# Gated attention and squared-ReLU MLP on one core: the exponent's shift from the first 512 keys, and the front part's steps in another order

## The chip, the cores and the metric

The kernel runs on 1 core of one Trainium2 chip. The metric is the device time of one execution in microseconds (us), as the median of several runs.

## The reference, cut to what matters

```python
x = A_x                                             # 1 x 2048 x 512
g = sigmoid((x * gate_w).sum(-1, keepdims=True))
q = (x @ wq) as 32 heads of 16;  k = x @ wk;  v = x @ wv      # one k and v for all heads
scores = einsum("bhqd,bkd->bhqk", q, k) * 16 ** -0.5
a = einsum("bhqk,bkd->bhqd", softmax(scores), v) @ wo
b = relu(x @ w1 + b1) ** 2 @ w2 + b2
out = g * a + (1 - g) * b
```

All of it is float32. wq and wk are drawn some 36 times larger than the other weights, so the scores spread widely.

## The kernel before, in words

The softmax does not look for the largest score of each row. It subtracts a bound, |q| times the greatest key norm, inside the score product itself: the key tile `k_aug` has, beside 3 x 16 rows of the key, a row RS = 32 that holds minus that norm (`km`), and the query tile `qa` has |q| in the same row. Both come twice, in partitions 0 to 48 and 64 to 112, for two heads side by side. A root is a guess from the exponent's bits (`k_max`, `root`). At the end the kernel tests whether every row's sum lay between `L_MIN` and `L_MAX` (2^-80 and 2^64); if one did not, `exact_shift` computes the attention anew.

The long middle part is an order of TensorE's work written by hand and by a planner. A *span* (`Span`, `fetch`) is one unit of products (a tile of queries, a hidden tile of the MLP, a sum): 12 or 15 matmuls in two halves of 64 rows. The second half of a unit runs beside the first half of the next, and each span starts a new PSUM bank `mm` (two of them). A *phase* places a few scores among the products by a text from `PLANS` (M a product, S0 a score block, 02 and 12 the two halves of a score block that goes through the PSUM bank `x` and is copied by VectorE). After each phase `context` multiplies finished exponentials with the values (`v_ext`, line 963). ScalarE turns scores into exponentials (line 943); VectorE copies, splits numbers into two float32r parts and takes units out of PSUM. `soon` lists VectorE's steps that are due early; `spend` lets them out when the planner's clock says that they fit.

The change is in the front part, lines 592 to 651, and in the first phase (`FIRST_PHASE`, line 62, and `last_rows`, line 653). For each chunk c of 512 keys:

- `kv_sums(c)`: x times wk and wv (four matmuls beside each other), then `kv_copy(c)` to SBUF on ScalarE.
- `k_rows(c)`: a matmul that spreads the keys into the rows of `k_aug`; `k_round(c)` rounds them (`kb`), `k_parts(c)` writes `k_aug` on VectorE; `k_shift(c)` then writes -km into row RS of both halves.
- `kv_gather(c)`, `kv_keep(c)`, `kv_turn(c)`: four small matmuls, a copy to SBUF and a transpose that put keys and values with one key a partition, in the PSUM bank `acc`. From there `k_squares` and `k_max` take the greatest norm, and `v_rows` writes `v_ext`.

The first query unit is made early (`q_early`); its rows go to `qa[0]` by small DMAs (`q_direct`) from the SP and POOL queues, and its norms (`qnorm`) as the last of them. `wq_load(2, 2)` loads the last two of the four tiles of wq, which `wq_round` and `wq_rest` split.

Two waits matter later. Each score block holds one of two PSUM buffers `s` until its exponential is done. And after the first phase a one-column copy on VectorE, `peek` (line 1394), reads the bank of the first span; TensorE's next products into that bank come behind it:

```python
        phase(span.slots, AHEAD + 2, 0)
        nc.vector.tensor_copy(at.tile([128, 1], F32, name="peek"), span.bank[:, :1])
        evicted = True
```

Of the kernel before, what the change touches and what calls it, by code (L numbers as in the profile page):

```python
# [10 lines left out]
F32 = mybir.dt.float32  # L11
# [11 lines left out]
NC, CH = 4, 512  # L23
# [37 lines left out]
}  # L61
FIRST_PHASE = "S0 M K M S1 M M M 02 M S3 M M M S4 M 12 M M S5", (0, 1, 3, 4, 5, 2)
HC = CH // 2

Q_ROWS = (0, 0, DH), (DH, 0, DH), (RS + 1, 1, DH), (RS, 2, 1)
FRONT_A, FRONT_V = 8, 22
LAST_OK = NC * KT - 1
# [105 lines left out]
def mix_kernel(ctx: ExitStack, tc: tile.TileContext, xT, xs, gw, wkv, wq, wo, w12, b1, b2, cst, out):  # L173
# [67 lines left out]
    with fast, tc.tile_pool(name="at", bufs=1) as at, \  # L241
# [43 lines left out]
        ones = at.tile([96, 128], BF, name="ones")  # L285
        kmx = at.tile([128, NK], F32, name="kmx")
        kmt = at.tile([128, 1], F32, name="kmt")
# [7 lines left out]
        for i in range(FRONT_V):  # L295
# [3 lines left out]
        ks = {}  # L299
        rows_of = {0: lambda: two[:, 0], 1: lambda: late_kv[:, 1], 2: aside,  # L300
                   3: lambda: mp.tile([128, CH], F32, name="mm")}
        kvt = [at.tile([128, 2, CH], F32, name="kvc", tag="e", bufs=10) for _ in range(2)]
# [3 lines left out]
        def kv_sums(c, parts=range(KT)):  # L306

            if parts[0] == 0:
                kvq[c] = late_kv[:, 0] if c == 3 else aside() if c == 1 else mp.tile([128, CH], F32, name="mm")
            for k in parts:  # L310
                nc.tensor.matmul(kvq[c][32 * k:32 * k + 32], wkvf[:, k], xf[c, k], start=True, stop=True,
                                 skip_group_check=True, tile_position=(0, 32 * k))
# [24 lines left out]

        ks2 = []
        kvg, gathered = [], {}

        def kv_gather(c):

            gathered[c] = mp.tile([128, CH], F32, name="mm") if c % 2 else aside()
            for j in range(4):
                nc.tensor.matmul(gathered[c][32 * j:32 * j + 32, :128], cs[:, C_SEL:C_SEL + 2 * DH],
                                 kvc[c][:, j * 128:(j + 1) * 128], start=True, stop=True,
                                 skip_group_check=True, tile_position=(0, 32 * j))

        def kv_keep(c):
            if not kvg:  # L350
                kvg.append(of_tile("kvg", F32))
            nc.scalar.activation(kvg[0][:, c * 128:(c + 1) * 128], gathered[c][:, :128], AF.Copy)

        def kv_turn(c):
            nc.tensor.transpose(acc[:, c * 128:(c + 1) * 128], kvg[0][:, c * 128:(c + 1) * 128], ident)

        def k_squares(i, n):
            if not ks2:
                ks2.append(of_tile("ksq", F32)[:, :NK * DH].rearrange("p (i d) -> p i d", i=NK))
            ksq = ks2[0]  # L360
            k = kvp[:, i:i + n, :DH]
            nc.scalar.activation(ksq[:, i:i + n], k, AF.Square)
            nc.vector.tensor_reduce(kmx[:, i:i + n], ksq[:, i:i + n], AX.X, OP.add)

        def k_max():
            nc.vector.tensor_reduce(kmt, kmx, AX.X, OP.max)
            pn = mp.tile([128, CH], F32, name="mm")
            nc.tensor.matmul(pn[:, :128], kmt.to_broadcast([128, 128]), ident, start=True, stop=True)

            def rest():  # L370
                nc.vector.tensor_reduce(km, pn[:, :128], AX.X, OP.max)
                nc.vector.tensor_scalar(km.bitcast(I32), km.bitcast(I32), 0.5, ROOT, op0=OP.mult, op1=OP.add)

            return rest

# [23 lines left out]
        def q_early():  # L399
            q = mp.tile([128, CH], F32, name="mm")  # L400
            mm(q, q_terms(0, 0))
            qr, ql = of_tile("qr"), of_tile("ql")

            def rest():
                nc.vector.tensor_tensor(ql, q, qr.bitcast(F32), OP.subtract)
                nc.vector.tensor_tensor(sq8[:, 0], qr.bitcast(F32), qr.bitcast(F32), OP.mult)

            return qr, ql, (lambda: nc.scalar.activation(qr, q, AF.Copy)), rest
# [26 lines left out]
        def qnorm(tiles, p8=None):  # L435
# [4 lines left out]
            for i, (it, sq) in enumerate(tiles):  # L440
                nc.tensor.matmul(p8[32 * i:32 * i + 32], blk, sq, start=True, stop=True, tile_position=(0, 32 * i))  # L441
            nrm, tmp = of_tile("nrm"), of_tile("tmp", F32)
            root(nrm[:n], p8[:n], tmp[:n])
            if tiles[0][0] == 0:
                q_direct(RS, nrm, 1, (nc.sync, nc.gpsimd))
            for i, (it, sq) in enumerate(tiles):
                nc.sync.dma_start(qs[2][it:it + 2].rearrange("u r d a n -> (u r d a) n"),
                                  nrm[32 * i:32 * i + 8].bitcast(F32))
                done.update((it, it + 1))
# [152 lines left out]
        x_pair(1, 0)  # L602
        kv_sums(1)
        two = sp.tile([128, 2, CH], F32, name="s")
        k_rows(0)
        nc.scalar.activation(xr[1][:, 2:], xw[1, 1], AF.Copy)  # L606
        q_round()
# [3 lines left out]
        q_direct(RS + 1, ql, DH, (nc.sync, nc.gpsimd))  # L611
        wq_load(2, 2)
        kv_copy(1)
        kv_gather(0)
        k_round(0)
        kv_keep(0)
        k_parts(0)
        kv_sums(2)
        qnorm([(0, sq8[:, 0])], mp.tile([128, CH], F32, name="mm"))
        kv_copy(2)  # L620
        acc = ap.tile([128, CH], F32, name="acc")
        kvp = acc.rearrange("p (i d) -> p i d", i=NK)
        kv_turn(0)
        kv_gather(1)
        kv_keep(1)
        kv_gather(2)
        kv_keep(2)
        nc.vector.tensor_tensor(xl[1][:, 2:], xw[1, 1], xr[1][:, 2:].bitcast(F32), OP.subtract)
        late_kv = sp.tile([128, 2, CH], F32, name="s")
        kv_sums(3)  # L630
        kv_copy(3)
        kv_turn(1)
        kv_turn(2)
        k_squares(0, 12)
        kv_gather(3)
        kv_keep(3)
        kv_turn(3)
        k_squares(12, 4)
        wq_round(1)
        k_rows(1)  # L640
        norm = k_max()
        nc.vector.tensor_copy(wqr[:, 2], wqf[2])
        k_rows(2)
        k_round(1)
        norm()
        k_shift(0, True)
        k_parts(1)
        k_round(2)
        k_parts(2)
        wq_rest(1)  # L650
        q_write(0, 0, qr, ql, nc.sync)

        def last_rows():

            nonlocal at_pe
            k_rows(3)
            k_round(3)
            k_parts(3)
            at_pe += 0.8
            act(0.6)  # L660
            dve(0.75)

        held, begun = 0.0, [0]
        chores, divisions = [], []
        soon = [(1, 0.7, lambda: wq_rest(2)), (1, 0.9, lambda: k_shift(1)), (1, 0.4, v_rows),
                (1, 0.7, lambda: (act(0.64), wq_round(3), wq_rest(3))), (2, 0.9, lambda: k_shift(2)), (3, 0.9, lambda: k_shift(3)),
# [630 lines left out]
        def phase(slots, n, m):  # L1297
# [23 lines left out]
            for i in range(len(rows[0])):  # L1321
                for r in range(2):
# [3 lines left out]
                    elif item == "K":  # L1326
                        if r == 0:
                            last_rows()
                    elif item[0] == "S":
# [157 lines left out]
```

## Time and profile before

| | |
|---|---|
| median of 3 runs | 1173.27 us (1173.03 to 1173.36) |
| the profiled execution | 1173.4 us, span 1171.8 us |
| TensorE (PE) busy | 1163.3 us, 99% |
| ScalarE (ACT) busy | 1022.9 us, 87% |
| VectorE (DVE) busy | 687.1 us, 59% |
| GpSimd (POOL) busy | 67.7 us, 6% |
| granted TensorE clock, mean | 0.999 |

The profile is of one execution. A timeline row gives the start and the length of one or several like instructions, and in square brackets how long the engine stood idle before and what ended that. Lines such as L906 are lines of the kernel. "PEld" are the weight loads of TensorE. A row with "POOLq" or "SPq" is a transfer issued from that queue; a row of the DMA view ends with the time from issue to landing, where the trace has it.

### The profile page before, as it was taken

How to read it: one execution, taken by the hardware profiler on the slowest of the kernel's cores; microseconds unless marked ns; L12 is line 12 of the kernel's file. 1: busy time of each engine (PE TensorE's matmuls, PEld its weight loads, DVE VectorE, ACT ScalarE, POOL GpSimd, SP SyncE). 2: the span in 40 equal slices, each digit the busy share in tenths (PEclk: the TensorE clock that was granted, in tenths of full speed). 3: DMA queues.
4: the chain of work that ended last, by engine and by line, in shares of the span. 5: the costliest groups of instructions: out<-in, count | busy, mean ns of one | idle time of the engine just before them, and what ended most of it. 6: DMA issues, size and time to landing. Idle time of an engine off the chain costs nothing.

```text
span 1171.8 us, 31969 instructions
## 1 busy us (share of the span) xinstructions
PE 1163.3 (99%) x13791; PEld 778.7 (66%) x13791; DVE 687.1 (59%) x1175; ACT 1022.9 (87%) x1142; POOL 67.7 (6%) x125
## 2 busy tenths in 40 slices
PE   8999999999999999999999999999999999999998
PEld 4666666676666666666666666666666666666665
DVE  6877886764754745553666636535556537544554
ACT  7789999999988888888888888989888889888885
POOL 1000111010100000100000000001000000001000
PEclk9999999999999999999999999999999999999999
DMA  7245535251533513320433305224115224222101
GB/s 265 98 156 175 183 114 195 92 197 45 176 119 121 180 39 121 110 81 20 151 104 143 95 22 180 92 66 157 62 47 168 79 66 136 92 75 92 56 38 39
DMA packets 49290, 130.26 MB, mean 111 GB/s; under 512 B 11350, under 2 KB 11846, under 8 KB 48632
## 3 DMA queue, kind: packets, MB, share of 16 engines
q1 hardware_dynamic: 37272, 90.68, 23.8%
q0 software_dynamic: 11728, 37.43, 8.8%
q8 instruction: 109, 1.79, 0.6%
q14 instruction: 37, 0.30, 0.1%
q10 hardware_dynamic: 144, 0.07, 0.0%
HBM read 87.92 MB, written 35.64 MB: 105 GB/s over the span
## 4 chain that ended last, share of the span: by engine, by line
PE 97%; DMA 1%; ACT 1%; SPq 0%; DVE 0%; issue 0%
PE acc L963 39%; PE mm L1270 34%; PE s L906 19%; PE x L906 5%; DMA xf<-in_xT 1%; DMA wqf<-in_wq 0%; ACT e L943 0%; DVE ot L1230 0%; SPq L413 0%; PE s L212 0%; SPq L268 0%; ACT xr L606 0%; PE mm L320 0%; PE x L1052 0%; PE x L441 0%
## 5 line engine op out<-in xcount | busy, mean ns | idle before, releaser
L943 ACT ACTIVATE e<-s 128x1024 f32<-128x1024 f32 x765 | 747.8, 1023 | 102.5 <-PE s L906 99.4
L927 DVE COPY e<-x 128x512 f32<-128x512 f32 x518 | 358.3, 692 | 445.0 <-PE x L906 275.9
L963 PE MATMUL acc<-e,v_ext 128*32 128x256 f32 x8192 | 470.2, 381 | 0.0
L906 PE MATMUL s<-qa,k_aug 49*128 49x512 f32 x1530 | 407.3, 410 | 0.5 <-DVE k_aug L336 0.3
L963 PEld LDWEIGHTS acc<-e,v_ext 128*32 128x32 f32 x8192 | 252.3, 110 | 193.1 <-issue 40.6
L943 ACT ACTIVATE e<-e 128x1024 f32<-128x1024 f32 x259 | 272.7, 1055 | 0.2 <-ACT e L943 0.2
L906 PEld LDWEIGHTS s<-qa,k_aug 49*128 49x128 f32 x1530 | 214.3, 184 | 85.1 <-ACT e L943 38.8
L1270 PE MATMUL mm<-w2p,hr 64*128 64x512 f32 x1128 | 242.1, 392 | 0.0
L906 PE MATMUL x<-qa,k_aug 49*128 49x512 f32 x518 | 213.5, 412 | 0.0
L1270 PEld LDWEIGHTS mm<-w2p,hr 64*128 64x128 f32 x1128 | 160.4, 186 | 18.5
L1270 PE MATMUL mm<-xragain,w1p 64*128 64x512 f32 x448 | 119.7, 392 | 0.0
L906 PEld LDWEIGHTS x<-qa,k_aug 49*128 49x128 f32 x518 | 95.2, 184 | 35.8 <-DVE e L927 19.8
L1270 PE MATMUL mm<-xr,w1p 64*128 64x512 f32 x448 | 114.8, 392 | 0.0
L1270 PEld LDWEIGHTS mm<-xragain,w1p 64*128 64x128 f32 x448 | 70.2, 186 | 6.7
L1270 PEld LDWEIGHTS mm<-xr,w1p 64*128 64x128 f32 x448 | 68.5, 186 | 6.9
L1270 PE MATMUL mm<-xlagain,w1p 64*128 64x512 f32 x224 | 69.6, 396 | 0.0
L1270 PE MATMUL mm<-xl,w1p 64*128 64x512 f32 x224 | 66.4, 393 | 0.0
L1270 PE MATMUL mm<-more 64*128 64x512 f32 x216 | 60.4, 394 | 0.0
L1017 ACT ACTIVATE accs<-acc 128x256 f32<-128x256 f32 x60 | 23.1, 384 | 28.8 <-PE acc L963 27.1
L789 DVE TENSOR_SCALAR big<-mm,b1t 128x512 f32<-128x512 f32 x56 | 41.6, 742 | 0.0
L790 DVE TENSOR_TENSOR big<-big 128x512 f32<-128x512 f32 x56 | 38.8, 692 | 1.9
L1270 PEld LDWEIGHTS mm<-xlagain,w1p 64*128 64x128 f32 x224 | 35.8, 186 | 4.0
(195 smaller groups left out, 804.0 us busy)
## 6 DMA issues: line engine op xcount, KB each, us to landing
w1p<-w1kept SPq DMA_DIRECT2D x42, 512.0 KB
w2p<-w2kept SPq DMA_DIRECT2D x35, 512.0 KB
qa<-qs SPq DMA_DIRECT2D x186, 64.0 KB
w1kept<-w1p POOLq DMA_DIRECT2D x14, 512.0 KB, 3.7
w2kept<-w2p POOLq DMA_DIRECT2D x12, 512.0 KB, 5.5
qs<-qr SPq DMA_DIRECT2D x16, 256.0 KB
ress<-res POOLq DMA_DIRECT2D x4, 1024.0 KB, 5.5
qs<-ql POOLq DMA_DIRECT2D x15, 256.0 KB, 3.7
```

Of the source, the lines that this page charges most:

```text
L789: nc.vector.tensor_scalar(h[0], p, b1t[:, f:f + 1], 0.0, op0=OP.add, op1=OP.max)
L790: nc.vector.tensor_tensor(h[0], h[0], h[0], OP.mult)
L906: nc.tensor.matmul(dst.rearrange("p (a n) -> p a n", a=2), k_aug[rows, kt * 128:(kt + 1) * 128], qa[it][rows, :, q * HC:q * HC + HC], star ...
L927: nc.vector.tensor_copy(e_half(u)[:, 2 * r:2 * r + 2], x.rearrange("p (a n) -> p a n", a=2))
L943: nc.scalar.activation(e_half(u), src, AF.Exp, scale=SCALE)
L963: nc.tensor.matmul(accs[q][h * 32:(h + 1) * 32], v_ext[:, kt], es[u][:, h % 2 * 2 + h // 2], start=kt == 0 and it > 0, stop=kt == NK - 1, ...
L1017: nc.scalar.activation(a[:, q * HC:q * HC + HC], acc, AF.Copy)
L1270: nc.tensor.matmul((self.before if r else self).bank, a[p], b[p], start=not r and i == 0, stop=r == 1 and i == len(self.terms[1]) - 1, ski ...
```

## The change

The greatest key norm is taken of the first chunk only, so `km` needs chunk 0 alone. In the front part only chunk 0 is gathered, kept and turned; chunks 1 to 3 are gathered, kept and turned inside the first phase, at two new places K of its text. The norms of the first queries come ahead of the root of the key norm. `wq_load(2, 2)` moves behind the norms' DMA on the SP queue. Three steps go from ScalarE to VectorE (the copy of the gathered chunks 1 to 3, the rounding of chunk 3's keys, the rounding of wq's tile 1), and VectorE's split of x's second chunk (`xl[1][:, 2:]`) moves from the front part into `soon`. The short fillers at the start are 5 instead of 8 on ScalarE and 20 instead of 22 on VectorE.

```diff
-FIRST_PHASE = "S0 M K M S1 M M M 02 M S3 M M M S4 M 12 M M S5", (0, 1, 3, 4, 5, 2)
+FIRST_PHASE = "S0 M M K S1 M M M 02 M S3 M K M M S4 M 12 M M K S5", (0, 1, 3, 4, 5, 2)
-FRONT_A, FRONT_V = 8, 22
+FRONT_A, FRONT_V = 5, 20
...
-        def k_squares(i, n):
...
+        def k_squares():
+            ksq = kvg[:, CH - 4 * DH:].rearrange("p (i d) -> p i d", i=4)
+            nc.scalar.activation(ksq, kvp[:, :4, :DH], AF.Square)
+            nc.vector.tensor_reduce(kmx, ksq, AX.X, OP.add)
             nc.vector.tensor_reduce(kmt, kmx, AX.X, OP.max)
...
+        def k_norm():
+            pn = acc[:, CH - 128:]
+            nc.tensor.matmul(pn, kmt.to_broadcast([128, 128]), ident, start=True, stop=True)
+            return pn
+
+        def k_root(pn):
+            nc.vector.tensor_reduce(km, pn, AX.X, OP.max)
+            nc.vector.tensor_scalar(km.bitcast(I32), km.bitcast(I32), 0.5, ROOT, op0=OP.mult, op1=OP.add)
...
+            if tiles[0][0] == 0:
+                k_squares()
             nrm, tmp = of_tile("nrm"), of_tile("tmp", F32)
             root(nrm[:n], p8[:n], tmp[:n])
             if tiles[0][0] == 0:
                 q_direct(RS, nrm, 1, (nc.sync, nc.gpsimd))
+                wq_load(2, 2)
...
         k_rows(0)
+        kv_gather(0)
...
-        wq_load(2, 2)
+        kv_keep(0, 1, scalar_copy)
+        k_round(0)
+        kv_sums(1)
+        kv_turn(0)
+        qnorm([(0, sq8[:, 0])])
         kv_copy(1)
...
+        pn = k_norm()
+        kv_sums(2)
+        kv_copy(2)
+        k_root(pn)
         k_parts(0)
...
+        k_shift(0, True)
         late_kv = sp.tile([128, 2, CH], F32, name="s")
+        k_rows(1)
+        k_round(1)
         kv_sums(3)
         kv_copy(3)
...
+        late_ks = mp.tile([128, CH], F32, name="mm")
+        nc.vector.tensor_copy(wqr[:, 1], wqf[1])
+        wq_rest(1)
         k_rows(2)
...
             k_rows(3)
-            k_round(3)
+            kb[3] = of_tile("kb")
+            nc.vector.tensor_copy(kb[3], ks[3])
             k_parts(3)
...
+        def v_gather():
+
+            for c in range(1, NC):
+                kv_gather(c)
+            kv_keep(1, 3, nc.vector.tensor_copy)
+
+        def v_turn():
+
+            for c in range(1, NC):
+                kv_turn(c)
+            v_rows()
+
+        aside_steps = [last_rows, v_gather, v_turn]
...
-        soon = [(1, 0.7, lambda: wq_rest(2)), (1, 0.9, lambda: k_shift(1)), (1, 0.4, v_rows),
+        soon = [(1, 0.7, lambda: (nc.vector.tensor_copy(wqr[:, 2], wqf[2]), wq_rest(2))),
+                (1, 0.9, lambda: k_shift(1)),
+                (1, 0.4, lambda: nc.vector.tensor_tensor(xl[1][:, 2:], xw[1, 1], xr[1][:, 2:].bitcast(F32), OP.subtract)),
...
-                            last_rows()
+                            aside_steps.pop(0)()
```

How the instructions stand on the engines, first TensorE between the early query unit and the first score block (`s<-qa,k_aug`). `mm<-xk,wkvf` and the like are `kv_sums`, `s<-kvc,cs` is `k_rows`, `32x128 x4` a `kv_gather`, `acc<-cs,kvg` a `kv_turn`, `cs,kmt` the norm. Before, behind `kv_sums(1)`, `k_rows(0)`, `kv_gather(0)`, `kv_sums(2)`, the queries' norms and `kv_turn(0)`:

```order
L345 MATMUL mm<-kvc,cs 32x128 x4
L345 MATMUL x<-kvc,cs 32x128 x4
L311 MATMUL s<-xk,wkvf 32x512 x4
L355 MATMUL acc<-cs,kvg 128x128 x2
L345 MATMUL mm<-kvc,cs 32x128 x4
L355 MATMUL acc<-cs,kvg 128x128
L320 MATMUL s<-kvc,cs 128x512
L368 MATMUL mm<-cs,kmt 128x128
L320 MATMUL x<-kvc,cs 128x512
L906 MATMUL s<-qa,k_aug 128x512 x2
```

And of the change, behind `k_rows(0)`:

```order
L340 MATMUL acc<-kvc,cs 32x128 x4
L310 MATMUL mm<-xf,wkvf 32x512 x4
L348 MATMUL acc<-cs,kvg 128x128
L430 LDWEIGHTS blk
L430 MATMUL x<-sq_172,blk 32x512
L358 MATMUL acc<-cs,kmt 128x128
L310 MATMUL mm<-xk,wkvf 32x512 x4
L319 MATMUL s<-kvc,cs 128x512
L310 MATMUL mm<-xk,wkvf 32x512 x4
L319 MATMUL x<-kvc,cs 128x512
L903 MATMUL s<-qa,k_aug 128x512 x2
```

The norm now stands ahead of the sums of chunks 2 and 3 and ahead of the rows of chunks 1 and 2, and three gathers and three transposes have left this place.

Second, VectorE from the last `k_parts` (`k_aug<-kb,cs,mm`) to `peek`. Before:

```order
L327 SCALAR_TENSOR_TENSOR k_aug<-kb,cs,mm 128x512
L564 TENSOR_TENSOR wql<-wqf,wqr 128x512
L927 COPY e<-x 128x512
L336 TENSOR_SCALAR k_aug<-km 1x512 x2
L927 COPY e<-x 128x512
L1394 COPY peek<-mm 128x1
```

And of the change, from the rounding of chunk 3's keys (`kb<-mm`, on ScalarE before) on:

```order
L638 CAST kb<-mm 128x512
L326 SCALAR_TENSOR_TENSOR k_aug<-kb,cs,mm 128x512
L660 CAST wqr<-wqf 128x512
L556 TENSOR_TENSOR wql<-wqf,wqr 128x512
L924 COPY e<-x 128x512
L345 COPY kvg<-acc 128x384
L335 TENSOR_SCALAR k_aug<-km 1x512 x2
L662 TENSOR_TENSOR xl_91<-xf,xr_87 128x1024
L924 COPY e<-x 128x512
L366 COPY v_ext<-acc 128x256
L1391 COPY peek<-mm 128x1
```

Five instructions that stood elsewhere, or on ScalarE, now stand ahead of `peek`.

Third, VectorE behind `peek`. Before (the copy to `v_ext` ahead of these rows):

```order
L564 TENSOR_TENSOR wql<-wqf,wqr 128x512
L336 TENSOR_SCALAR k_aug<-km 1x512 x4
L204 CAST xr_88<-xk 128x512
L205 TENSOR_TENSOR xl_92<-xk,xr_88 128x512
L422 CAST qr<-mm 128x512
L423 TENSOR_TENSOR ql<-mm,qr 128x512
```

And of the change:

```order
L556 TENSOR_TENSOR wql<-wqf,wqr 128x512
L335 TENSOR_SCALAR k_aug<-km 1x512 x4
L204 CAST xr_88<-xk 128x512
L205 TENSOR_TENSOR xl_92<-xk,xr_88 128x512
L204 CAST xr_88<-xk 128x512
L205 TENSOR_TENSOR xl_92<-xk,xr_88 128x512
L411 CAST qr<-mm 128x512
L412 TENSOR_TENSOR ql<-mm,qr 128x512
```

One more split of x (`xr`, `xl`) stands ahead of the two steps that take the second query unit out of its bank. From the second span on TensorE's order is the same as before to the end.

## Rows read from the trace of the kernel before

**Rows 1.** The page: the span, TensorE's busy time and its granted clock

```profile
span 1171.8 us, 31969 instructions
...
PE 1163.3 (99%) x13791; PEld 778.7 (66%) x13791; DVE 687.1 (59%) x1175; ACT 1022.9 (87%) x1142; POOL 67.7 (6%) x125
...
PEclk9999999999999999999999999999999999999999
```

**Rows 2.** The timeline of TensorE in the front part (start, length, instruction)

```profile
10.69 1.06 PE L311 MATMUL x<-xf,wkvf 128*32 128x512 f32 x8
...
12.74 0.42 PE L345 MATMUL x<-kvc,cs 128*32 128x128 f32 x8
...
16.96 0.43 PE L345 MATMUL mm<-kvc,cs 128*32 128x128 f32 x8 [0.35 <-ACT kvc L315]
...
18.98 0.46 PE L368 MATMUL mm<-cs,kmt 128*128 128x128 f32 x2
19.27 1.02 PE L320 MATMUL x<-kvc,cs 128*128 128x512 f32 x2
20.62 0.70 PE L906 MATMUL s<-qa,k_aug 49*128 49x512 f32 x2 [0.32 <-DVE k_aug L336]
```

**Rows 3.** The timeline of TensorE from the first phase to the third span

```profile
21.27 1.12 PE L320 MATMUL mm<-kvc,cs 128*128 128x512 f32 x2
...
26.74 0.50 PE L1270 MATMUL mm<-xr,wqr 64*128 64x512 f32 x1 [0.21 <-DVE peek L1394]
...
29.99 0.50 PE L906 MATMUL s<-qa,k_aug 49*128 49x512 f32 x2 [0.20 <-ACT e L943]
...
31.66 2.80 PE L963 MATMUL acc<-e,v_ext 128*32 128x256 f32 x48
...
34.38 0.19 PEld L1270 LDWEIGHTS mm<-xr,wqr 64*128 64x128 f32 x2 [0.41 <-DVE ql L423]
```

**Rows 4.** The timeline of VectorE in the front part and the first phase

```profile
14.26 0.68 DVE L381 TENSOR_SCALAR tmp<-mm 32x512 int32<-32x512 int32 x1
14.97 0.42 DVE L382 CAST nrm<-tmp 32x512 fp32r<-32x512 f32 x1
15.31 1.21 DVE L628 TENSOR_TENSOR xl<-xf,xr 128x1024 fp32r<-128x1024 f32 x1
...
19.30 0.43 DVE L642 CAST wqr<-wqf 128x512 fp32r<-128x512 f32 x1 [0.47 <-DMA wqf<-in_wq]
19.64 0.28 DVE L371 TENSOR_REDUCE km<-mm 128x1 f32<-128x128 f32 x1
...
23.06 0.75 DVE L327 SCALAR_TENSOR_TENSOR k_aug<-kb,cs,mm 128x512 fp32r<-128x512 f32 x1 [0.29 <-ACT kb L324]
...
24.33 0.68 DVE L927 COPY e<-x 128x512 f32<-128x512 f32 x1
...
26.54 0.15 DVE L1394 COPY peek<-mm 128x1 f32<-128x1 f32 x1
26.60 0.42 DVE L377 COPY v_ext<-acc 128x256 f32<-128x256 f32 x1
```

**Rows 5.** The timeline of VectorE behind the first phase

```profile
29.06 0.69 DVE L564 TENSOR_TENSOR wql<-wqf,wqr 128x512 fp32r<-128x512 f32 x1 [2.04 <-ACT wqr L561]
...
33.29 0.69 DVE L423 TENSOR_TENSOR ql<-mm,qr 128x512 fp32r<-128x512 f32 x1
```

**Rows 6.** The timeline of POOL's queue: the issue of the first norms' row

```profile
15.68 0.53 POOL L413 DMA_DIRECT2D qa<-nrm  x1 [2.27 <-DVE nrm L382]
```

**Rows 7.** The DMA view of the first 45 us (count, size, us to landing)

```profile
qs<-ql POOLq DMA_DIRECT2D x2, 256.0 KB, 3.3
...
qa<-ql POOLq DMA_DIRECT2D x1, 64.0 KB, 5.1
...
qa<-nrm POOLq DMA_DIRECT2D x1, 4.0 KB, 3.8
```

**Rows 8.** Windows: busy time of each engine from 40 to 50 us

```profile
40.00:50.00 10.00, 10.00 (x129) 6.84 (x123) 8.17 (x15) 7.22 (x9) 1.29 (x2) 1.00 0.27 107
```

More of the change, by code (lines that the diff above doesn't have):

```diff
@@ L285, in mix_kernel @@
         ones = at.tile([96, 128], BF, name="ones")
-        kmx = at.tile([128, NK], F32, name="kmx")
+        kmx = at.tile([128, 4], F32, name="kmx")
         kmt = at.tile([128, 1], F32, name="kmt")
@@ L299, in mix_kernel @@
         ks = {}
-        rows_of = {0: lambda: two[:, 0], 1: lambda: late_kv[:, 1], 2: aside,
-                   3: lambda: mp.tile([128, CH], F32, name="mm")}
+        rows_of = {0: lambda: two[:, 0], 1: lambda: late_kv[:, 0], 2: aside, 3: lambda: late_ks}
         kvt = [at.tile([128, 2, CH], F32, name="kvc", tag="e", bufs=10) for _ in range(2)]
@@ L308, in kv_sums @@
             if parts[0] == 0:
-                kvq[c] = late_kv[:, 0] if c == 3 else aside() if c == 1 else mp.tile([128, CH], F32, name="mm")
+                kvq[c] = mp.tile([128, CH], F32, name="mm")
             for k in parts:
@@ L336, in k_shift @@
                     nc.vector.tensor_scalar(row, src, -1.0, None, op0=OP.mult)
-        ks2 = []
-        kvg, gathered = [], {}
         def kv_gather(c):
-            gathered[c] = mp.tile([128, CH], F32, name="mm") if c % 2 else aside()
             for j in range(4):
-                nc.tensor.matmul(gathered[c][32 * j:32 * j + 32, :128], cs[:, C_SEL:C_SEL + 2 * DH],
+                nc.tensor.matmul(acc[32 * j:32 * j + 32, c * 128:(c + 1) * 128], cs[:, C_SEL:C_SEL + 2 * DH],
                                  kvc[c][:, j * 128:(j + 1) * 128], start=True, stop=True,
@@ L347, in kv_gather, with kv_keep @@
                                  skip_group_check=True, tile_position=(0, 32 * j))
[L349 to L352, printed above, removed]
+        def kv_keep(c, n, copy):
+            copy(kvg[:, c * 128:(c + n) * 128], acc[:, c * 128:(c + n) * 128])
         def kv_turn(c):
-            nc.tensor.transpose(acc[:, c * 128:(c + 1) * 128], kvg[0][:, c * 128:(c + 1) * 128], ident)
@@ L357, in k_squares @@
-        def k_squares(i, n):
[L358 to L365, printed above, removed]
-            nc.vector.tensor_reduce(kmt, kmx, AX.X, OP.max)
[L367 to L374, printed above, removed]
+            nc.tensor.transpose(acc[:, c * 128:(c + 1) * 128], kvg[:, c * 128:(c + 1) * 128], ident)
@@ L404, in rest @@
             def rest():
+                nc.vector.tensor_tensor(sq8[:, 0], qr.bitcast(F32), qr.bitcast(F32), OP.mult)
                 nc.vector.tensor_tensor(ql, q, qr.bitcast(F32), OP.subtract)
-                nc.vector.tensor_tensor(sq8[:, 0], qr.bitcast(F32), qr.bitcast(F32), OP.mult)
             return qr, ql, (lambda: nc.scalar.activation(qr, q, AF.Copy)), rest
@@ L602, in mix_kernel @@
         x_pair(1, 0)
-        kv_sums(1)
         two = sp.tile([128, 2, CH], F32, name="s")
+        kvg = of_tile("kvg", F32)
+        acc = ap.tile([128, CH], F32, name="acc")
+        kvp = acc.rearrange("p (i d) -> p i d", i=NK)
         k_rows(0)
+        kv_gather(0)
         nc.scalar.activation(xr[1][:, 2:], xw[1, 1], AF.Copy)
@@ L611, in mix_kernel @@
         q_direct(RS + 1, ql, DH, (nc.sync, nc.gpsimd))
-        wq_load(2, 2)
+        kv_keep(0, 1, scalar_copy)
[3 more added lines that the diff above has]
+        qnorm([(0, sq8[:, 0])])
         kv_copy(1)
-        kv_gather(0)
-        k_round(0)
-        kv_keep(0)
+        pn = k_norm()
+        kv_sums(2)
+        kv_copy(2)
+        k_root(pn)
         k_parts(0)
[L618 to L628, printed above, removed]
+        k_shift(0, True)
         late_kv = sp.tile([128, 2, CH], F32, name="s")
+        k_rows(1)
+        k_round(1)
         kv_sums(3)
         kv_copy(3)
[L632 to L642, printed above, removed]
+        late_ks = mp.tile([128, CH], F32, name="mm")
+        nc.vector.tensor_copy(wqr[:, 1], wqf[1])
+        wq_rest(1)
         k_rows(2)
-        k_round(1)
-        norm()
-        k_shift(0, True)
         k_parts(1)
@@ L649, in mix_kernel @@
         k_parts(2)
-        wq_rest(1)
         q_write(0, 0, qr, ql, nc.sync)
```

## The prediction

> **What bounds the kernel now.** The page first: TensorE is busy 1163.3 us of the span of 1171.8 us at a granted clock of 9 tenths or more in every slice [rows 1], and in the stretch from 40 to 50 us it is busy 10.00 of 10.00 us [rows 8]. So a change gains only what it takes from TensorE's idle time or work, and the work is the same here: the change moves matmuls, it removes none but the few columns that the smaller norm doesn't square. What is to be had lies in the front. There I read TensorE's timeline, then VectorE's, to see who was late at each start. Three points matter. The first score block starts at 20.62 us, after a wait for `k_aug` [rows 2]: call it T0. The second phase starts at 26.74 us, after a wait for `peek` [rows 3], which VectorE runs at 26.54 [rows 4]. The third span starts at 34.38 us, where the row names `ql`, VectorE's second step on the second query unit [rows 3, 5]. Behind that, TensorE's order is that of before and its idle time is nil, so **the shift of the third span is the shift of the end**.
>
> **How the first scores move.** TensorE is free for `k_rows(0)` at 10.69 us, where `kv_sums(1)` started. One `k_rows` lasts 1.02 us [rows 2], so the gather of chunk 0 starts at about 11.7. From the last gather to the norm's matmul it was 16.96 to 18.98, 2.02 us [rows 2]. The same copy, transpose, square and two reductions follow now, but `kv_sums(1)` stands ahead of the transpose; a sums and a rows together take 2.05 us (10.69 to 12.74 [rows 2]), so it is 1.03 us, part of which lies beside the copy. I add 0.4 of it: the norm at 14.1 us, some 4.9 us earlier than before.
>
> Most of that is used up at once. VectorE now makes the queries' norms ahead of the root, 0.68 + 0.42 us [rows 4], so `km` is begun at about 15.1. It was 0.98 us from there to the first score (19.64 [rows 4] to 20.62 [rows 2]), and chunk 0's `k_parts`, 0.75 us [rows 4], now stands in between: the keys are ready at 16.9. TensorE is not: behind the norm come 0.29 us of its own (18.98 to 19.27) and twice sums and rows, 4.10 us, so it reaches the score at 18.5 at the latest [rows 2]. Third, the norms' row. `nrm` ends at 15.1; POOL issued it 0.29 us after its end (15.39 to 15.68 [rows 4, 6]), so now at 15.4. The same 4 KB took 3.8 us to land, behind a transfer that took 5.1; an issue from the same queue in calmer traffic took 3.3 [rows 7]. So it lands at 18.7 to 19.2. I take T0 = 18.8, near the lower end, since the load of half a MB of wq now starts behind the norms and not ahead of them. The ends for T0 are 18.2 (TensorE with its steps closer together, the row early) and 19.2. **The first score comes about 1.8 us earlier.**
>
> The DMA row can be read against the Trainium skill, "DMA: Bandwidth & Descriptors", section "Anatomy of one DMA — SWDGE (gpsimd) path", which gives such a transfer a fixed cost of about 2.0 us; the 3.8 us of the row is nearly twice that. By the page the row would land at 17.4 us, TensorE alone would set T0, and the sum below would be 0.3 to 0.6 us smaller.
>
> **Where it is given back: VectorE up to `peek`.** Before, VectorE needed 3.48 us from the last `k_parts` to `peek` (23.06 to 26.54 [rows 4]). All of that stays, and five steps join it, each on the way to `peek`: rounding chunk 3's keys, priced as the copy of the same shape out of PSUM, 0.68; wq's tile 2, 0.43; the copy of the gathered chunks, three quarters of 0.68, say 0.5; the split of x, 1.21; the copy to `v_ext`, 0.42 [rows 4]. That is 3.24 us more, 6.7 in all. The first of them starts when TensorE has done `k_rows(3)`, which started 0.65 us behind T0 and lasted 1.12 [rows 2, 3]; one more product stands ahead of it, say 0.3 (half of that 0.65): T0 + 2.1 = 20.9. So `peek` is at 27.6, against 26.54: **1.1 us later**, though the first score is 1.8 us earlier. Between ready work and `peek` TensorE stands: its first phase took 20.62 to 26.53 with 5.9 us, and now has three gathers of 0.42 and three small transposes more, so it is done between 24.7 and 26.8, and idles 1 to 3 us where it idled 0.2.
>
> **What comes back behind `peek`.** Before, VectorE stood 2.04 us ahead of `wql` [rows 5], waiting for a rounding on ScalarE that was behind in its exponentials; TensorE also waited for an exponential at 29.99 (0.20 shown [rows 3]). ScalarE now has three steps fewer and the later `peek` lets it catch up. `wql` came 2.5 us behind `peek`; between no wait (0.2) and as before (2.5) I take 1.3, since one exponential and one rounding still follow VectorE's second copy. From `wql` to the end of `ql` it was 4.9 us (29.06 to 33.98 [rows 5]); one more split of x stands there, 0.43 + 0.69 [rows 4, 5]. So `ql` ends 1.3 + 6.0 = 7.3 us behind `peek`. TensorE itself took 7.84 us from `peek` to the third span (26.54 to 34.38 [rows 3, 4]); without the waits on ScalarE some 0.4 to 0.6 less, 7.2 to 7.4. Both say 7.4: the third span at 27.6 + 7.4 = 35.0, against 34.38.
>
> **The other edits.** The fillers at the start end while their engines wait for x, so their number costs nothing. wq's tile 1 rounded on VectorE (0.43) lies behind the keys of chunk 0 and ahead of `k_rows(3)`, where TensorE is the later one; if it weren't, it would cost its 0.43 at `peek`. The load of wq's tiles 2 and 3 is issued about 2 us later than at 13.64, and its first use moves from 19.30, where it was awaited [rows 4], to 21 or later: nothing on the path. The smaller shift changes numbers only.
>
> **The sum.** The profiled execution took 1173.4 us. +0.6 us at the third span gives 1174.0; the median of the runs is 0.13 below the profiled one, so I forecast **1173.9 us**. The bounds: T0 of 18.2 and 19.2 give 0 and +1.0; `peek` to the third span, 7.2 to 8.5, gives -0.2 and +1.1. Together 1173.0 to 1175.4 in the corners.
>
> **The rivals.**
> - *The early start reaches the end.* If the split of x or the copies didn't hold `peek` (VectorE quicker than the sum of its rows, or TensorE not really held there), the end would come 1.8 us earlier, up to 2.4: 1171.5, at best 1170.9. For it: the first score's gain is solid. Against: VectorE's order is fixed, and the row at 26.74 shows TensorE waiting for just that instruction [rows 3]. 6%.
> - *The norms' row lands late.* With the 5.1 us of its neighbour [rows 7] it would land at 20.5, T0 would be as before and all that joined VectorE would count in full: +2.3, 1175.6. It decides against the kernel from a landing of 20.5 on. 4%.
> - *TensorE's clock falls in the gap ahead of `peek`* (slower). So far the granted clock is at its upper level throughout [rows 1], with waits of some tenths of a us [rows 2, 3]; a gap of 1 to 3 us is new. If the level fell to 1.2 GHz there, the second phase (26.74 to 31.66, 4.9 us [rows 3]) would run at half the rate until it rises: +2.4 to +4.9, so 1177 us or so. It decides from the gap at which the level falls, which no row shows. The Trainium skill, "TensorE: Matmul & The Clock Gate", Part 1, says that the array's clock is held at half by default and that only activity releases it; by that rule a standstill ahead of `peek` is the place to look. 5%.
> - *The fallback runs.* A shift too small for later chunks could push sums out of their bounds and have the attention computed anew, at hundreds of us. From the reference's inputs, the greatest key norm is 13.72 in all and 13.44 in the first 512 keys; the sums then lie between 2^-38.9 and 2^-3.5, far inside. Under 1%.
>
> **How the numbers follow.** A difference of 0.2%, 2.35 us, is about what can be told from none. The forecast, with all of its bounds, has 84%, and lies within 0.2%. Of the early start a third would count as faster, and some of the unforeseen: 3%. Slower are the clock, half of the late row and the fallback: 7%. The range takes in the bounds and most of the late row and leaves out the rest: 1172.2 to 1175.2.
>
> **What the profile of the change would show.** Right: the first score near 18.8 us, its wait ended by the POOL transfer or none; VectorE without a gap from the rounding of chunk 3's keys to `peek`; `peek` near 27.6 and TensorE idle 1 to 3 us ahead of it; `wql` behind `peek` with less than 2.04 us of wait; the third span near 35.0; all else as before. Wrong: `peek` ahead of 26.5 (then the gain is real), a first score at 20 or later, a granted clock below its upper level near 27 us, or TensorE idle behind the third span.

## The result and the profile after

The changed kernel takes **1175.85 us** (median of 18 runs, 1174.38 to 1176.37), the kernel before on the same chip 1173.40 us (18 runs, 1173.03 to 1174.21). The ratio is 1.0017 with a 95% interval of 1.0010 to 1.0024: slower, by about the 0.2% that the prediction took as the limit of what can be told, with an interval that leaves out 1. The forecast of 1173.9 us was 2 us too low, and 1175.85 lies above its range.

The 18 times are not one heap. Eight lie from 1174.38 to 1174.93 us (mean granted clock 1.000 in seven, 0.999 in one), ten from 1175.78 to 1176.37 us (0.998 or 0.999), and nothing lies in the 0.85 us between. (The mean clock by itself is too coarse to sort runs by: the kernel before has 0.999 and 1.000 too.) The median is the low edge of the upper group. The profiled execution, 1174.61 us with a span of 1173.1, belongs to the lower one. So there are two questions: where 1.2 us came from in the profiled run, and what some 1.5 us more the others have.

The page of the changed kernel, span and busy times, answers to [rows 1]:

```profile
span 1173.1 us, 31962 instructions
...
PE 1164.3 (99%) x13791; PEld 781.3 (67%) x13791; DVE 688.1 (59%) x1175; ACT 1020.9 (87%) x1133; POOL 67.9 (6%) x125
...
PEclk9999999999999999999999999999999999999999
```

Of the span's 1.3 us more, 1.0 is busy time of TensorE, with the same count of matmuls, and the weight loads (PEld) are busy for 2.6 us more. The forty slices of 29 us are too coarse to show a clock that falls for some us.

TensorE's timeline of the changed kernel (start, length, instruction, idle time before), to be laid beside [rows 2, 3]:

```profile
18.74 0.70 PE L903 MATMUL s<-qa,k_aug 49*128 49x512 f32 x2 [0.18 <-issue]
...
26.06 0.40 PE L1267 MATMUL mm<-xr,wqr 64*128 64x512 f32 x1
27.69 0.49 PE L1267 MATMUL mm<-xr,wqr 64*128 64x512 f32 x1 [1.23 <-DVE peek L1391]
...
32.20 2.80 PE L960 MATMUL acc<-e,v_ext 128*32 128x256 f32 x48
35.04 0.50 PE L1267 MATMUL mm<-xr,wqr 64*128 64x512 f32 x2
...
1162.30 1.93 PE L960 MATMUL acc<-e,v_ext 128*32 128x256 f32 x32
```

And VectorE's, beside [rows 4, 5]:

```profile
17.04 0.43 DVE L625 CAST wqr<-wqf 128x512 fp32r<-128x512 f32 x1 [0.67 <-DMA wqf<-in_wq]
...
20.89 0.69 DVE L638 CAST kb<-mm 128x512 fp32r<-128x512 f32 x1 [0.92 <-PE mm L319]
...
25.41 1.23 DVE L662 TENSOR_TENSOR xl<-xf,xr 128x1024 fp32r<-128x1024 f32 x1
...
27.48 0.15 DVE L1391 COPY peek<-mm 128x1 f32<-128x1 f32 x1
28.99 0.69 DVE L556 TENSOR_TENSOR wql<-wqf,wqr 128x512 fp32r<-128x512 f32 x1 [1.35 <-ACT wqr L553]
...
34.29 0.69 DVE L412 TENSOR_TENSOR ql<-mm,qr 128x512 fp32r<-128x512 f32 x1
```

The front went as forecast. The first score starts at 18.74 (20.62 before), VectorE then works from 20.89 to `peek` with no gap that the view shows, `peek` is at 27.48 (26.54 before), TensorE's last matmul ahead of it starts at 26.06 and the next waits 1.23 us, and the third span starts at 35.04 (34.38 before): **+0.66 us**.

But the end is later than that. Before, the last context block of this kind started at 1161.10:

```profile
1161.10 1.93 PE L963 MATMUL acc<-e,v_ext 128*32 128x256 f32 x32
```

Now it is at 1162.30, 1.20 us later, of which 0.66 came with the third span. From the third span to this block it was 1126.72 us and is now 1127.26. That **+0.54 us** lies behind the third span, where the order of TensorE's work is that of before. TensorE shows no wait there: the windows view (stretch, length, busy time and count of PE, PEld, DVE, ACT, POOL, granted clock, DMA share, GB/s) of the kernel before reads

```profile
40.00:1160.00 1120.00, 1120.00 (x13473) 755.44 (x13469) 652.95 (x1088) 991.66 (x1094) 63.96 (x115) 1.00 0.32 108
```

and that of the changed kernel

```profile
40.00:1160.00 1120.00, 1120.00 (x13461) 757.70 (x13457) 651.94 (x1086) 991.67 (x1093) 64.20 (x115) 1.00 0.33 108
```

TensorE is busy all of the 1120 us in both, and in the same time the changed kernel gets 12 matmuls fewer done (some only because the stretch ends at another place of its order), while its weight loads are busy for 2.26 us more. Busy time is the time in which at least one load runs, and loads overlap. The single load is as long as before, as one large group shows, first of the kernel before and then of the changed one (behind the first bar the busy us of the group over the whole span and the mean ns of one):

```profile
L1270 PEld LDWEIGHTS mm<-w2p,hr 64*128 64x128 f32 x1128 | 160.4, 186 | 18.5
L1267 PEld LDWEIGHTS mm<-w2p,hr 64*128 64x128 f32 x1128 | 161.4, 186 | 17.2
```

So both kernels keep the array busy, and the changed one is a little slower at the same work; no single instruction shows why.

### The profile page after: what moved, and what is told of

It is laid out like the page before. It is cut to its first block, busy times and chain, and to the rows that moved or that the text cites. A ratio compares the mean times of both kernels' runs of the same rounds, so it can differ in the third digit from the quotient of the medians.

```text
span 1173.1 us, 31962 instructions
## 1 busy us (share of the span) xinstructions
PE 1164.3 (99%) x13791; PEld 781.3 (67%) x13791; DVE 688.1 (59%) x1175; ACT 1020.9 (87%) x1133; POOL 67.9 (6%) x125
## 4 chain that ended last, share of the span: by engine, by line
PE 97%; DMA 2%; DVE 1%; SPq 0%; issue 0%; ACT 0%
PE acc L960 39%; PE mm L1267 34%; PE s L903 19%; PE x L903 5%; DMA wqf<-in_wq 1%; DMA rows<-in_xs 1%; DVE ot L1227 0%; PE s L212 0%; DVE xl L662 0%; PE x L1049 0%; PE x L430 0%; SPq L268 0%; DVE wql L556 0%; PE mm L1084 0%; DVE e L924 0%; SPq L678 0%
## 5 line engine op out<-in xcount | busy, mean ns | idle before, releaser
L1267 PEld LDWEIGHTS mm<-w2p,hr 64*128 64x128 f32 x1128 | 161.4, 186 | 17.2
L1267 PE MATMUL mm<-wor,orr 64*128 64x512 f32 x120 | 38.4, 395 | 0.0
```

Source lines behind the costliest of these rows:

```text
L1267: nc.tensor.matmul((self.before if r else self).bank, a[p], b[p], start=not r and i == 0, stop=r == 1 and i == len(self.terms[1]) - 1, ski ...
```

## The experiments

Four explanations were tried, by the letters of the expectations. **A**: in part of the runs TensorE's clock falls in the gap ahead of `peek`. **B**, its rival: the lower mean clock is only the tail behind the last matmul, and the slower runs lose their time at some other wait. **C**: the tile `kmx` has become narrower (16 columns to 4, 48 bytes a partition), so the tiles behind it in SBUF have moved, and TensorE's reads with them. **D**: the squares of the keys no longer take a tile of their own from the ring of `of_tile`, so later tiles lie elsewhere in that ring. Each kernel was timed in 5 rounds, 11 runs; the kernel before had medians of 1173.36, 1173.32 and 1173.37 us beside them on the three chips used; single runs of it went up to 1175.01 us at a mean clock of 1.000, so that one high run proves nothing by itself.

The results in one table. "Behind it" is the time from the start of the third span to the last context block, less the 1126.72 us of before, both columns from the one profiled run.

| kernel | median us (range) | ratio (95%) | third span | behind it |
|---|---|---|---|---|
| e1 the changed kernel again | 1175.79 (1174.44-1176.61) | 1.0017 (1.0007-1.0026) | 36.34 | +0.80 |
| e2 x split early | 1174.56 (1174.30-1175.26) | 1.0010 (1.0001-1.0019) | 34.72 | +0.58 |
| e3 gap filled | 1174.59 (1174.43-1175.35) | 1.0011 (1.0002-1.0020) | 34.80 | +0.67 |
| e4 before, `peek` later | 1176.36 (1174.81-1177.32) | 1.0024 (1.0015-1.0033) | 37.30 | +0.13 |
| e5 `kmx` wide | 1173.89 (1173.44-1175.18) | 1.0006 (0.9997-1.0015) | 34.80 | +0.22 |
| e6 squares in the ring | 1175.98 (1174.36-1176.46) | 1.0020 (1.0011-1.0029) | 36.67 | +0.66 |
| e7 two steps moved | 1173.76 (1173.55-1175.12) | 1.0005 (0.9996-1.0014) | 34.45 | +0.46 |
| e8 before, a pad | 1174.61 (1174.25-1175.13) | 1.0009 (1.0000-1.0018) | 34.96 | +0.71 |
| e9 gap filled, `kmx` wide | 1174.01 (1173.46-1174.89) | 1.0004 (0.9995-1.0013) | 35.50 | +0.31 |
| e10 e7 with `kmx` wide | 1173.15 (1172.61-1173.31) | 0.9996 (0.9987-1.0005) | 33.85 | +0.01 |

### e1: the changed kernel, unaltered

> The changed kernel unaltered. Its 18 runs fall in two groups, 1174.4 to 1174.9 us (8 runs, mean granted clock 0.999 to 1.000) and 1175.8 to 1176.4 us (10 runs, 0.998 to 0.999). Theory A (the gap): TensorE's wait of 1.2 us for peek now and then makes the clock fall to its lower level for a while near 28 to 32 us; then about half of the runs are again near 1176, each with a lower mean clock than the others, and a profile of one shows the fall in that stretch. Theory B (the end): the lower mean clock is only the tail behind the last matmul, and the 1.5 us come from somewhere else, a DMA or a queue; then a slow profile shows the clock at its upper level up to the tail, and the time is lost at a wait.

Four runs lie from 1174.44 to 1174.66 us (mean clock 1.000), seven from 1175.67 to 1176.61 (0.999). With the 18 runs of the result, 17 of 29 are in the upper group. This time the profiled run (1176.25 us) is one of them. Its windows, the same columns as above:

```profile
26.00:27.00 1.00, 0.32 (x3) 0.00 (x0) 1.00 (x2) 0.80 (x1) 0.00 (x0) 1.00 0.08 29
27.00:28.00 1.00, 0.45 (x4) 0.41 (x6) 0.49 (x3) 0.97 (x2) 0.00 (x0) 1.00 0.00 0
28.00:29.00 1.00, 1.00 (x8) 0.74 (x6) 0.14 (x1) 0.83 (x2) 0.00 (x0) 0.52 0.00 0
29.00:30.00 1.00, 1.00 (x8) 0.80 (x6) 0.97 (x3) 0.00 (x0) 0.00 (x0) 0.50 0.00 0
...
31.00:32.00 1.00, 1.00 (x10) 0.77 (x10) 0.94 (x3) 0.41 (x2) 0.00 (x0) 0.77 0.00 0
32.00:33.00 1.00, 0.98 (x9) 0.51 (x5) 0.97 (x3) 1.00 (x2) 0.00 (x0) 1.00 0.00 0
```

The same stretch of the changed kernel's first profile, a run of the lower group:

```profile
26.00:27.00 1.00, 0.46 (x3) 0.01 (x1) 1.00 (x2) 0.67 (x1) 0.00 (x0) 1.00 0.01 4
27.00:28.00 1.00, 0.31 (x2) 0.30 (x4) 0.63 (x3) 0.97 (x2) 0.00 (x0) 1.00 0.00 0
28.00:29.00 1.00, 1.00 (x12) 0.80 (x10) 0.01 (x1) 0.95 (x2) 0.00 (x0) 1.00 0.00 0
```

TensorE has done the same in both: less than half busy from 26 to 28, with one standstill of 1.23 us. In e1 the granted clock then falls to its lower level, 1.2 GHz, early in the us from 28 (0.52 is half rate for 0.96 of it), and rises in the us from 31. Eight matmuls fit into a us there, and 12 at 2.4 GHz. Two rows of e1's TensorE timeline, the second phase and the third span, give the price:

```profile
27.55 0.49 PE L1267 MATMUL mm<-xr,wqr 64*128 64x512 f32 x1 [1.23 <-DVE peek L1391]
...
36.34 0.50 PE L1267 MATMUL mm<-xr,wqr 64*128 64x512 f32 x2
```

From the second phase to the third span it took 8.79 us (27.55 to 36.34), against 7.35 (27.69 to 35.04): **1.44 us for the fall**. It begins while TensorE is already working again: a wait that is over is paid for afterwards. B is out, since the clock falls and the time is lost here and not at the end.

### e2: the split of x out of `peek`'s way

```diff
         late_ks = mp.tile([128, CH], F32, name="mm")
+        nc.vector.tensor_tensor(xl[1][:, 2:], xw[1, 1], xr[1][:, 2:].bitcast(F32), OP.subtract)
         nc.vector.tensor_copy(wqr[:, 1], wqf[1])
...
-                (1, 0.4, lambda: nc.vector.tensor_tensor(xl[1][:, 2:], xw[1, 1], xr[1][:, 2:].bitcast(F32), OP.subtract)),
```

> The changed kernel with x's second split (1.23 us on VectorE) moved ahead of the cast of wq's tile 1, where VectorE stands 0.67 us for a DMA and 0.37 and 0.92 us later on. My theory (VectorE's queue ahead of peek holds TensorE): peek moves from 27.48 to about 26.3, TensorE's gap of 1.23 us shrinks to 0.2 or less, the third span comes 0.7 to 1.2 us earlier, and the median is 1173.3 to 1173.8 with no run near 1176. Rival (the split costs the same wherever it stands, or the first scores wait for it): peek stays within 0.3 us of 27.5 and the time within 0.5 us of the changed kernel's.

The step of 1.23 us fits into the gaps that VectorE had ahead of 20.89, and `peek` comes at 26.06. The second phase follows with no wait that the view shows, and no run lies in the upper group: right. The time was expected at 1173.3 to 1173.8 us and is 1174.56. Rows of e2's VectorE timeline show where the 1.4 us by which `peek` came earlier went:

```profile
26.06 0.15 DVE L1391 COPY peek<-mm 128x1 f32<-128x1 f32 x1
...
28.67 0.69 DVE L556 TENSOR_TENSOR wql<-wqf,wqr 128x512 fp32r<-128x512 f32 x1 [2.45 <-ACT wqr L553]
```

and a row of its TensorE timeline, the start of the third span:

```profile
34.72 0.50 PE L1267 MATMUL mm<-xr,wqr 64*128 64x512 f32 x2 [0.66 <-DVE ql L412]
```

`wql` still waits for ScalarE's rounding, now 2.45 us instead of 1.35, so it starts only 0.32 us earlier. `ql` is late behind it, and TensorE waits 0.66 us at the third span. A gain at `peek` is lost again at the next point of waiting. The rest of the profiled run's time (1174.31 us) is the +0.58 behind the third span, which this edit does not touch. Five of the 11 runs lie apart from the others, at 1174.93 to 1175.26 us against at most 1174.56, with a mean clock of 1.000 in four of them; what they lose is not known.

### e3: the gap filled with idle work

```diff
+                    if spans == 2 and not r and i == 0:
+                        for _ in range(6):
+                            nc.tensor.matmul(self.bank, a[p], b[p], start=True, stop=False, skip_group_check=True)
                     nc.tensor.matmul((self.before if r else self).bank, a[p], b[p], start=not r and i == 0,
```

> The changed kernel with the first product of the second span issued six times more, into the bank that it starts anyway, so that TensorE works in the gap ahead of peek (six times 0.23 us, beside the wait of 1.23 us for peek). Theory A (clock): all runs are near 1174.5 to 1174.9, the group near 1176 is gone, and the mean clock is that of the faster group. Theory B: the two groups stay, at 1174.6 and 1176.1. If the wait itself were not the limit, six products would add 1.4 us to every run.

The first product behind the gap is issued six times more, ahead of `peek` (each overwrites the bank, so the six are idle work). In e3's windows TensorE is busy where it stood before:

```profile
26.00:27.00 1.00, 1.00 (x6) 0.79 (x6) 1.00 (x3) 0.91 (x1) 0.00 (x0) 1.00 0.03 10
27.00:28.00 1.00, 1.00 (x7) 0.62 (x7) 0.44 (x3) 0.97 (x2) 0.00 (x0) 1.00 0.00 0
28.00:29.00 1.00, 1.00 (x11) 0.80 (x11) 0.25 (x1) 0.72 (x2) 0.00 (x0) 1.00 0.00 0
```

Ten of the 11 runs lie from 1174.43 to 1174.82 and one at 1175.35: the upper group is gone, though `peek` (27.29) and the third span (34.80) are within 0.2 us of where they were. (The mean clock, 0.999 in seven runs and 1.000 in four, was expected to be that of the lower group and is too coarse to tell.) That shows A. Nothing was gained on the path: the wait for `peek` is still paid, and what the work in it takes away is the clock's part alone.

### e4: the same gap put into the kernel before

```diff
         phase(span.slots, AHEAD + 2, 0)
+        for _ in range(13):
+            nc.vector.memset(front[:, 1:], 0.0)
         nc.vector.tensor_copy(at.tile([128, 1], F32, name="peek"), span.bank[:, :1])
```

> The kernel before with thirteen one-column memsets (0.125 us each, 1.6 us) on VectorE ahead of peek and nothing else. If a wait at peek is enough by itself: peek at 28.2 instead of 26.54, TensorE's wait there 1.8 us instead of 0.2, part of it given back behind (VectorE then waits less for ScalarE's rounding), so the faster runs at 1173.9 to 1174.8; by theory A a second group of runs some 1.5 us above these with a lower mean clock, by theory B none.

Thirteen memsets hold `peek` to 28.29 us. Ten of 11 runs are now at 1175.93 to 1177.32 us (mean clock 0.997 to 0.999), one at 1174.81 (1.000). The windows of e4:

```profile
27.00:28.00 1.00, 0.00 (x0) 0.00 (x0) 0.47 (x8) 0.97 (x2) 0.00 (x0) 1.00 0.66 254
...
29.00:30.00 1.00, 1.00 (x8) 0.81 (x6) 0.70 (x2) 0.25 (x1) 0.00 (x0) 0.50 0.00 0
```

So the kernel before has the same weakness as soon as it stands there: 1.75 us of wait ahead of 28.50, the fall behind it, and 1.6 us from the one run without it to the middle of the others (1176.4). The gap alone costs +1.45 in that one run (1174.81 against 1173.36), at the upper end of what was expected. Behind the third span it is +0.13, near before: its tiles have not moved.

### e5: `kmx` as wide as it was

```diff
-        kmx = at.tile([128, 4], F32, name="kmx")
+        kmx = at.tile([128, NK], F32, name="kmx")[:, :4]
```

> The changed kernel with the little tile kmx as wide as before (16 columns, 4 of them used), so that every tile behind it in SBUF lies where it lay before. In the profiles the changed kernel loses 0.5 to 0.7 us more, spread over the whole span behind the third span, a few ns in each stretch of products and scores, whether or not the clock fell. Theory C (the places of tiles, shifted by 48 bytes a partition, make TensorE's products a little slower): the spread loss goes below 0.2 us and the faster runs come at 1173.9 to 1174.1. Rival (something else, such as the other order of VectorE's or the ring's steps): the runs stay in the two groups at 1174.5 and 1176.0.

No instruction is another; only the tile is wider, and 12 of its columns are never used. The median falls to 1173.89 us. Nine runs lie from 1173.44 to 1174.04 and two at 1175.09 and 1175.18. The middle of the nine, 1173.86, is 0.6 to 0.7 us below those of the changed kernel's lower groups (1174.45 in the first runs, 1174.60 in e1). Busy times on e5's page:

```profile
PE 1163.8 (99%) x13791; PEld 778.8 (66%) x13791; DVE 688.2 (59%) x1175; ACT 1020.5 (87%) x1133; POOL 67.9 (6%) x125
```

The windows view of e5, the same stretch as above:

```profile
40.00:1160.00 1120.00, 1120.00 (x13469) 755.35 (x13465) 652.31 (x1087) 991.58 (x1094) 64.15 (x115) 1.00 0.33 108
```

The busy time of the weight loads is back where it was before (778.7), eight matmuls more than in the changed kernel are done in the 1120 us, and +0.54 behind the third span has become +0.22. This is C. What it leaves open: the gap ahead of `peek` is there as before (1.29 us), yet the clock seems to have fallen in two of 11 runs only (those 1.2 to 1.3 us above the middle of the rest, mean clock 0.998 and 0.999), not in 17 of 29. At that rate two or fewer of 11 would come by chance about once in a hundred times (an estimate), and e6, on the same chip with `kmx` narrow, has nine of 11. So most of the 1.96 us by which the median is lower than the changed kernel's is falls of the clock that did not come, and why they did not is not shown.

### e6: the squares in a tile of the ring again

```diff
-            ksq = kvg[:, CH - 4 * DH:].rearrange("p (i d) -> p i d", i=4)
+            ksq = of_tile("ksq", F32)[:, :4 * DH].rearrange("p (i d) -> p i d", i=4)
```

> The changed kernel with the squares in a tile of their own from the ring of ten (as before), and not at the end of kvg, so that every later tile of that ring (query parts, hidden parts) has the place in the ring that it had before. Theory D (the rotated ring is what spreads the loss of 0.5 to 0.7 us over the span): faster runs at 1173.9 to 1174.1. Rival: the two groups at 1174.5 and 1176.0 as before.

Two runs at 1174.36 and 1174.66, nine at 1175.89 to 1176.46; +0.66 behind the third span, weight loads busy for 782.0 us. D falls: the ring's order is not the cause.

### e7: two steps moved on VectorE

```diff
+        nc.vector.tensor_tensor(xl[1][:, 2:], xw[1, 1], xr[1][:, 2:].bitcast(F32), OP.subtract)
         nc.vector.tensor_copy(wqr[:, 1], wqf[1])
...
         nc.vector.tensor_copy(at.tile([128, 1], F32, name="peek"), span.bank[:, :1])
         evicted = True
+        for c in (2, 3):
+            dve(0.9)
+            k_shift(c)
```

> The changed kernel with x's second split in VectorE's early gap (as in the run with that edit alone) and, behind peek, the shifts of chunks 2 and 3 (four writes, 1.72 us) ahead of the wait for ScalarE's rounding of wq's tile 3, where VectorE stood 2.45 us in that run. If the third span is then held by VectorE's queue no more: its first product at about 34.0 instead of 34.72 us (before: 34.38), no wait for ql, no fall of the clock, and, with the spread loss of 0.5 to 0.6 us still there, a median of 1173.5 to 1174.0. If the wait for ql stays, it is the rounding on ScalarE that holds it, and the time is that of the run with x's split alone, 1174.5.

This is e2 with the shifts of chunks 2 and 3 taken out of the list `soon` and written behind `peek`, where VectorE waits for ScalarE's rounding anyway. `wql` then waits 0.75 us, no wait for `ql` is shown, and the third span is at 34.45, 0.07 us from before. The time, 1173.76 us, is as expected; what is left of the loss is the +0.46 behind the third span.

### e8: the kernel before with its tiles moved

```diff
         kmx = at.tile([128, NK], F32, name="kmx")
+        pad = at.tile([128, 4], F32, name="pad")
+        nc.vector.memset(pad, 0.0)
```

> The kernel before with a tile of 4 columns (16 bytes a partition) put behind kmx and written once, so that every tile behind it in SBUF lies 16 bytes further, which is the same remainder of 64 as the 48 bytes less of the changed kernel. Theory C (places of tiles): the front part is as before (first score 20.6, third span 34.4), the loss is spread over the span, 0.4 to 0.6 us in all, and the median is 1173.7 to 1174.0. Rival (it was the width of kmx in another way, or chance): 1173.3 as before.

The kernel before loses 1.24 us (1174.61 against 1173.37), by more than was expected and in another way. The load of wq's tiles is awaited 0.88 us instead of the 0.47 of [rows 4], the third span is at 34.96, and of the +0.71 behind it two single steps (0.33 us near 168 us and 0.39 near 1060) make nearly all. The weight loads are busy for 778.4 us, not more. So moving tiles by 16 bytes, or the one memset more, changes the time of this kernel by over 1 us, but it does not copy what the changed kernel shows. C rests on the three pairs with a narrow and a wide `kmx`, not on this run.

### e9 and e10: both repairs together

e9 is e3's and e5's edit together, e10 e7's and e5's.

> The changed kernel with both cures: six more products in the gap ahead of peek (no fall of the clock) and kmx as wide as before (no spread loss). What is left is what VectorE's queue ahead of peek and behind it costs, 0.4 us at the third span: a median of 1173.6 to 1173.9, all runs in one group. If the three causes do not add up, it lies at 1174.3 or above, or in two groups.

> The run with x's second split early and the shifts of chunks 2 and 3 ahead of the wait behind peek, and kmx as wide as before. By theory C the spread loss of 0.45 us goes, and with the third span within 0.1 us of the kernel before the median is 1173.1 to 1173.4, the same as the kernel before. Rival: 1173.7 as without the wide tile.

e9: one group, 1173.46 to 1174.89, no fall in its profile; the median 1174.01 is 0.1 us above what was expected. Its profiled run is the slowest of the 11 (third span at 35.50). e10 came as expected, 1173.15 us, and is 2.7 us below the changed kernel. Busy times on its page:

```profile
PE 1163.6 (99%) x13791; PEld 779.7 (67%) x13791; DVE 688.0 (59%) x1175; ACT 1019.9 (87%) x1133; POOL 68.1 (6%) x125
```

The third span and the last context block in its TensorE timeline:

```profile
33.85 0.50 PE L1267 MATMUL mm<-xr,wqr 64*128 64x512 f32 x2
...
1160.58 1.94 PE L960 MATMUL acc<-e,v_ext 128*32 128x256 f32 x32
```

The third span is 0.53 us ahead of before, the last context block 0.52: now the shift of the one is the shift of the other. Against the kernel before it is a draw (0.2 us, ratio 0.9996, interval 0.9987 to 1.0005). The three pairs that differ in the width of `kmx` alone agree: wide is faster by 0.6 to 0.7 us in e5 (lower groups), by 0.58 in e9 against e3 and by 0.61 in e10 against e7. The two of each pair ran on different chips, on which the kernel before differs by 0.05 us at most. The column "behind it" agrees as well: +0.46 to +0.80 in the six profiles with a narrow `kmx`, +0.01 to +0.31 in the four with a wide one and no pad (e4, e5, e9, e10). The two profiles of the one changed kernel differ by 0.26 there, so a single one is not to be read finer than that.

## Why the prediction failed, point by point

**What held.** The first score (18.8 forecast, 18.74 measured), `peek` (27.6, 27.48), TensorE's gap ahead of it (1 to 3 us, 1.23 in the one wait), the step back to the third span (35.0, 35.04), with VectorE the engine that gives the early start back. `wql` was forecast 1.3 us behind `peek` and came 1.5 behind, with 1.35 us of wait where [rows 5] had 2.04. POOL issued the norms' row at 15.17 (15.4 forecast); it took 3.5 us to land, so 18.7, level with the first score. The Trainium skill's 2.0 us ("DMA: Bandwidth & Descriptors", section "Anatomy of one DMA — SWDGE (gpsimd) path") would have had it there by 17.2, an estimate by that page; the twelve profiles show 2.5 to 4.2 us, none as quick, so the row of before was the better source. The late row is worth some 0.3 us: where it took at most 2.9 us (e1, e2, e3, e9, e10), the first score starts 1.05 or 1.06 us behind the start of the `k_rows` ahead of it, with no wait, and in the changed kernel's first profile 1.31 us (17.43 to 18.74). The early start's rival (6%) and the late row's (4%) did not come.

**What failed first: the chance of the clock's fall.** The step "TensorE's clock falls in the gap ahead of `peek`" had 5%; it was true in 17 of 29 runs, by their times and by the rows of the one of them that was profiled, and it sets the median. The argument for 5% was that the granted clock had been at its upper level throughout, with waits of some tenths of a us. That is no evidence on a standstill of over 1 us, which the same text forecast; with no row on either side, the chance should have been nearer to even. The prediction's own sign of being wrong, a granted clock below its upper level near 27 us, is what e1 shows from 28.04 us on. The price was off the other way: +2.4 to +4.9 were forecast for a second phase run wholly at half rate, and it was 1.44 us, since the clock fell only when the phase had begun and rose before its end. The rule that was cited there, of the Trainium skill, "TensorE: Matmul & The Clock Gate", Part 1, that the array's clock is halved by default and only activity releases it, agrees with e1's rows (0.50 behind the standstill) and with e3's (1.00 with the standstill filled); the changed kernel's first profile, at 1.00 behind the same standstill, shows that the fall is not certain.

**What failed second: "behind that, TensorE's order is that of before", so the third span's shift is the end's.** The order is, but not the speed: 0.54 us more came in the stretch in which TensorE never waits. The term that was missing stands under "The other edits": the smaller norm was said to change columns and numbers only, but it also changes where the tiles behind `kmx` lie. With the old width, +0.54 becomes +0.22 (e5), and +0.46 becomes +0.01 (e10). That the width of this tile brings the loss is shown by e5, whose instructions are those of the changed kernel, and by the two other pairs; nothing else that is known changes with it but the places of the tiles behind it. By what mechanism TensorE becomes slower is not shown: the single weight load is as long in both, and e8 says that it is no simple rule.

**The sum, mended.** 1173.4 of the profiled run before, +0.66 at the third span and +0.54 behind it, is 1174.6: the profiled run (1174.61) and the lower group. With +1.44 for the clock it is 1176.0: the upper group, ten of 18 runs, at whose low edge the median stands.

## What to carry to other kernels

A change that puts a standstill of more than a us in front of a busy matmul engine is to be costed twice, by the wait and by the clock that can fall behind it, and its times are to be read one by one: two groups with a space between them say that something happens in part of the runs, which one profile may not show. If the wait cannot go, idle matmuls in it (e3) take away the second cost and leave the first. And in a kernel that is busy 99% of the span, leave the places of tiles alone while you measure something else: a resized tile of a few bytes is a change of its own, to be tried by itself.

## What the chip showed unexpectedly

- A wait of 1.23 us, with TensorE 0.31 to 0.46 busy in each of the two us around it, was followed by a granted clock of 1.2 GHz in one of two profiles and, by the times, in 17 of 29 runs; one of 1.75 us in 10 of 11; and one of 1.29 us, with `kmx` wide, in perhaps 2 of 11. The fall came about half a us after the work had begun again (28.04 against 27.55 in e1), and ended in the us from 31.
- Narrowing one small tile by 48 bytes a partition went with 2.6 us more in which weight loads were busy (778.7 to 781.3), though the single load was as long as before (186 ns); widening it again without using the room brought that back (778.8 in e5), and 0.6 to 0.7 us of the time, with the same instructions.
- A tile of 16 bytes and one memset more cost the kernel before 1.24 us (e8), by a later third span and two single steps. The memset was not tried alone, so which of the two it was stays open.
